# Sliding-window attention with features on the partitions: QK summed by column-tiled selector matmuls, softmax weights spread over the features by DMA

## The chip, the cores and the metric

The kernel runs on one core of one Trainium2 chip. The metric is device time in microseconds (us) of one launch. Every number below comes from the listed runs or from the profile of one execution; "fast" is the state of a run whose time lies within 1.5% of the fastest run of the same kernel.

Engines are named as in the profile: PE (TensorE matmul), PEld (its weight loads), DVE (VectorE), ACT (ScalarE), POOL (GpSimd), SP (SyncE, which issues most DMAs), and the core's 16 DMA engines. A "granted clock" is the TensorE clock that the throttle allowed.

## The reference, cut to what matters

Two layers, each an attention part and a token-mixing MLP, over x of 2048 tokens and 1024 features in bf16. The MLP is not touched by the change.

```python
H = 32; Dh = D // H            # 32 heads of 32 features
W, dil = 8, 2                  # each token sees 8 keys: itself and 7 earlier ones, two apart
qkv = (x @ wqkv) ...           # q, k, v
idx = pos[:, None] - off[None, :]          # off = arange(W) * dil
logits = einsum("bhsd,bhswd->bhsw", q, kg) * scale      # kg = k gathered at idx
logits = where(mask, logits, -1e9)
attn = softmax(logits, axis=-1)
o = einsum("bhsw,bhswd->bhsd", attn, vg)
x = x + o.transpose(...).reshape(B, S, D) @ wo
```

Because the dilation is 2, even and odd tokens never meet in attention. Both kernels treat them as two classes of 1024 tokens each.

## The kernel before

Tokens lie on the partitions (8 per partition and class), and features on the free axis. A chunk is 8 heads of one class; there are 8 chunks a layer. DVE multiplies q with the eight shifted k, then halves the 32 features three times by adds. The rest of that sum, the softmax and the multiplication with v (PV in what follows, as QK is the one with k) follow on DVE too. Because the probability of a token and head lies on the same partition as the features it weights, the multiplication with v reads it through a broadcast along the free axis, without any copy. PE fills DVE's time with projections and MLP matmuls, which an emission loop weaves in between.

```python
def qk(self, ci):                                    # 8 heads (QW = 256 features), 8 tokens a partition
    ...
    for u0 in range(0, W, WB):                       # WB = 2 windows at a time
        nc.vector.tensor_tensor(out=flat, in0=qb, in1=windows(k, u0, WB, [(1, J * QW)]), op=ALU.mult)
        nc.vector.tensor_tensor(out=pr[:, :, 0:16, :], in0=pr[:, :, 0:16, :], in1=pr[:, :, 16:32, :], op=ALU.add)
        nc.vector.tensor_tensor(out=pr[:, :, 0:8, :], in0=pr[:, :, 0:8, :], in1=pr[:, :, 8:16, :], op=ALU.add)
        nc.vector.tensor_tensor(out=St[...], in0=pr[:, :, 0:4, :], in1=pr[:, :, 4:8, :], op=ALU.add)
        yield 0.0, 4.9

def weighted(self, ci, u0, n, dst):                  # PV: the weight is broadcast along the free axis
    v = windows(v_t[ci % 2], u0, n, [(QW, J), (HQ, DH), (1, HQ)])
    pw = Pb[:, u0:u0 + n].unsqueeze(3).to_broadcast([P, n, J, DH, HQ])
    nc.vector.tensor_tensor(out=dst..., in0=v, in1=pw, op=ALU.mult)
```

## Time and profile before

The kernel takes 1396.39 us (median of 4 runs, 1395.99 to 1400.52). The profiled execution spans 1394.9 us.

| Stage | us | PE busy | DVE busy |
|---|---|---|---|
| attention, layer 0 | 0 to 388 | 353 of 388 | 335 of 388 |
| MLP, layer 0 | 388 to 620 | 231 of 232 | 65 |
| attention, layer 1 | 620 to 1066 | 405 of 446 | 364 of 446 |
| MLP, layer 1 | 1066 to 1395 | 325 of 329 | 54 |

The page of the kernel before opens with the busy time of the engines. In the slices, each digit is the busy share of a fortieth of the span, in tenths. The two last lines are the chain of waits that ended last.

```profile
PE 1314.1 (94%) x7840; PEld 749.7 (54%) x7840; DVE 818.0 (59%) x928; ACT 483.4 (35%) x940; POOL 10.5 (1%) x20
...
PE   6999989999899999999899989899949999999998
...
DVE  4869999999820433327999939929976023211111
...
DMA  9423224532342226653365554334206222243531
...
PE 56%; DVE 35%; ACT 6%; issue 2%; DMA 2%; SPq 0%; DVEq 0%; ACTq 0%
```

PE is nearly full everywhere, and in the two attention stages DVE is busy for 86% and 82% as well. A change pays only if it takes work from both there, or moves it to something that has room.

The groups of instructions of the kernel before (busy us, then the mean ns of one) price what the change removes and keeps. L289 and L290 are two of the three QK tree adds, L288 is a QK multiplication (there are two such groups), and L321 a PV multiplication.

```profile
L289 DVE TENSOR_TENSOR T_126<-T_126 128x2048 bf16<-128x2048 bf16 x64 | 78.1, 1221 | 1.2
L288 DVE TENSOR_TENSOR T_126<-q_117,k_119 128x4096 bf16<-128x4096 bf16 x32 | 73.1, 2284 | 4.1 <-PE psg L336 2.2
L321 DVE TENSOR_TENSOR T_126<-v_121,Pb 128x4096 bf16<-128x4096 bf16 (+1 forms) x40 | 73.8, 1864 | 0.9
L290 DVE TENSOR_TENSOR T_126<-T_126 128x1024 bf16<-128x1024 bf16 x64 | 44.0, 688 | 1.4
```

### The profile page before, as it was taken

The numbers are of one execution on the slowest core, as the hardware profiler recorded it, in microseconds if no ns is written. First come the engines' busy times: TensorE is split into PE (matmuls) and PEld (weight loads), VectorE is DVE, ScalarE is ACT, GpSimd is POOL, SyncE is SP. The second block draws the span as 40 slices with busy tenths as digits, with TensorE's granted clock in tenths as the row PEclk, the third lists the DMA queues.
The fourth block names the chain that finished last, engine by engine and source line by source line (L and its number), as shares of the span: only waits on it lengthen the run. The fifth ranks groups of instructions, "written<-read, shape, count | busy, mean of one in ns | idle before, by whom it ended". The sixth has DMA issues, their size and how long they took to land.

```text
span 1394.9 us, 18742 instructions
## 1 busy us (share of the span) xinstructions
PE 1314.1 (94%) x7840; PEld 749.7 (54%) x7840; DVE 818.0 (59%) x928; ACT 483.4 (35%) x940; POOL 10.5 (1%) x20
## 2 busy tenths in 40 slices
PE   6999989999899999999899989899949999999998
PEld 5777656654344444458665458664414444444443
DVE  4869999999820433327999939929976023211111
ACT  7953348633122430013244543475312134100000
POOL 3000000000000000000000000000000000000000
PEclk9999999999999999999999999999969999999999
DMA  9423224532342226653365554334206222243531
GB/s 244 122 72 95 77 66 129 169 94 73 102 136 80 79 72 197 184 156 115 109 172 160 154 162 114 105 102 136 83 16 181 70 81 73 82 137 99 150 99 57
DMA packets 230916, 160.50 MB, mean 115 GB/s; under 512 B 7632, under 2 KB 208336, under 8 KB 230832
## 3 DMA queue, kind: packets, MB, share of 16 engines
q1 hardware_dynamic: 230720, 159.30, 39.3%
q8 instruction: 61, 1.00, 0.3%
q0 software_dynamic: 112, 0.01, 0.1%
q14 instruction: 23, 0.19, 0.0%
HBM read 127.94 MB, written 16.78 MB: 104 GB/s over the span
## 4 chain that ended last, share of the span: by engine, by line
PE 56%; DVE 35%; ACT 6%; issue 2%; DMA 2%; SPq 0%; DVEq 0%; ACTq 0%
PE psg L488 11%; PE pso L488 9%; PE psg L466 9%; DVE T_126 L321 8%; PE ps L273 7%; DVE T_126 L288 7%; PE pso L433 6%; PE pso L466 5%; PE ps L466 4%; DVE T_126 L289 4%; DVE o_q L350 3%; DVE T_126 L349 3%; DVE T_126 L290 2%; DVE St L291 1%; DVE xo L493 1%
## 5 line engine op out<-in xcount | busy, mean ns | idle before, releaser
L433 PE MATMUL pso<-wo,oT 128*128 128x512 bf16 x512 | 121.5, 389 | 0.7 <-DVE xn L439 0.4
L288 DVE TENSOR_TENSOR T_126<-q_116,k_118 128x4096 bf16<-128x4096 bf16 x32 | 73.2, 2289 | 55.5 <-ACT q_116 L275 36.4
L493 DVE SCALAR_TENSOR_TENSOR xo<-psg,b_sb,xs 128x512 bf16<-128x512 f32 x32 | 24.0, 749 | 124.6 <-PE psg L488 124.6
L493 DVE SCALAR_TENSOR_TENSOR xo<-pso,b_sb,xs 128x512 bf16<-128x512 f32 x32 | 24.0, 750 | 103.9 <-PE pso L488 98.6
L433 PEld LDWEIGHTS <-oT 128*128 128x128 bf16 x512 | 50.4, 100 | 62.2 <-issue 7.5
L321 DVE TENSOR_TENSOR T_126<-v_120,Pb 128x4096 bf16<-128x4096 bf16 (+1 forms) x40 | 74.0, 1864 | 11.7 <-PE psg L336 10.8
L289 DVE TENSOR_TENSOR T_126<-T_126 128x2048 bf16<-128x2048 bf16 x64 | 78.1, 1221 | 1.2
L288 DVE TENSOR_TENSOR T_126<-q_117,k_119 128x4096 bf16<-128x4096 bf16 x32 | 73.1, 2284 | 4.1 <-PE psg L336 2.2
L321 DVE TENSOR_TENSOR T_126<-v_121,Pb 128x4096 bf16<-128x4096 bf16 (+1 forms) x40 | 73.8, 1864 | 0.9
L477 DVE TENSOR_TENSOR tmp<-pso,g_132 128x512 f32<-128x512 f32 x4 | 2.8, 692 | 117.0 <-DMA w_10309<-in_B_w_dram 60.7
L273 PE MATMUL ps<-wq,hT_152 128*128 128x256 bf16 x384 | 51.4, 288 | 4.7 <-DMA wq<-in_A_wqkv_dram 2.1
L273 PE MATMUL ps<-wq,hT_6303 128*128 128x256 bf16 x384 | 46.5, 280 | 4.6 <-ACT v_120 L275 4.2
L273 PE MATMUL ps<-wq,hT_4874 128*128 128x256 bf16 x384 | 46.5, 280 | 4.5 <-ACT v_120 L275 4.1
L357 PE MATMUL tpo<-ident,o_q 128*128 128x128 bf16 x256 | 23.9, 235 | 27.9 <-DVE o_q L350 26.2
L358 ACT COPY oT<-tpo 128x1024 bf16<-128x1024 bf16 x32 | 32.3, 1010 | 47.3 <-PE tpo L357 47.3
L273 PE MATMUL ps<-wq,hT_153 128*128 128x256 bf16 x384 | 44.9, 273 | 3.1 <-ACT hT_153 L244 2.5
L273 PEld LDWEIGHTS <-hT_152 128*128 128x128 bf16 x384 | 38.9, 103 | 14.3 <-ACT hT_152 L244 2.9
L273 PE MATMUL ps<-wq,hT_810 128*128 128x256 bf16 x384 | 44.9, 273 | 1.7 <-ACT q_117 L275 1.0
L273 PE MATMUL ps<-wq,hT_811 128*128 128x256 bf16 x384 | 45.5, 273 | 0.4 <-ACT v_120 L275 0.4
L290 DVE TENSOR_TENSOR T_126<-T_126 128x1024 bf16<-128x1024 bf16 x64 | 44.0, 688 | 1.4
L350 DVE TENSOR_TENSOR o_q<-o_q,T_126 128x2048 bf16<-128x2048 bf16 x36 | 44.1, 1225 | 1.2
L349 DVE TENSOR_TENSOR T_126<-T_126 128x2048 bf16<-128x2048 bf16 x36 | 44.1, 1224 | 1.1
(1405 smaller groups left out, 2629.3 us busy)
## 6 DMA issues: line engine op xcount, KB each, us to landing
wq<-in_A_wqkv_dram SPq DMA_DIRECT2D x48, 512.0 KB, 4.2
wo<-in_A_wo_dram SPq DMA_DIRECT2D x64, 128.0 KB, 2.7
xr<-in_A_x_dram SPq DMA_DIRECT2D x16, 256.0 KB, 3.1
out_dram<-xo SPq DMA_DIRECT2D x16, 256.0 KB, 2.2
k_118<-k_118 SPq DMA_DIRECT2D x8, 392.0 KB, 5.0
v_120<-v_120 SPq DMA_DIRECT2D x8, 392.0 KB, 5.0
k_119<-k_119 SPq DMA_DIRECT2D x8, 392.0 KB, 5.0
v_121<-v_121 SPq DMA_DIRECT2D x8, 392.0 KB, 4.9
```

Source lines behind the costliest of these rows:

```text
L273: nc.tensor.matmul(ps[:, jj, :], lhsT=self.hT[c][j // JH][:, kt, j % JH, :], rhs=wts[part][:, kt, :], start=(kt == 0), stop=(kt == KD - 1))
L288: nc.vector.tensor_tensor(out=flat, in0=qb, in1=windows(k, u0, WB, [(1, J * QW)]), op=ALU.mult)
L289: nc.vector.tensor_tensor(out=pr[:, :, 0:16, :], in0=pr[:, :, 0:16, :], in1=pr[:, :, 16:32, :], op=ALU.add)
L290: nc.vector.tensor_tensor(out=pr[:, :, 0:8, :], in0=pr[:, :, 0:8, :], in1=pr[:, :, 8:16, :], op=ALU.add)
L321: nc.vector.tensor_tensor(out=dst.rearrange("p u j (d h) -> p u j d h", h=HQ), in0=v, in1=pw, op=ALU.mult)
L349: nc.vector.tensor_tensor(out=tf[:, 0], in0=tf[:, 0], in1=tf[:, 1], op=ALU.add)
L350: nc.vector.tensor_tensor(out=of, in0=of, in1=tf[:, 0], op=ALU.add)
L358: nc.scalar.copy(out=oT[:, b, :, :], in_=tp[:])
L433: nc.tensor.matmul(ps[:], lhsT=at_.oT[c][kt // 2][:, kt % 2, j, :], rhs=wo_t[n][kt // 4][:, kt % 4, :], start=(kt == 0), stop=(kt == KD - ...
L466: nc.tensor.matmul(ps[:], lhsT=wt[c][:, j, fl * P:(fl + 1) * P], rhs=h2[c][j // JH][:, j % JH, dc * 512:(dc + 1) * 512], start=(k == 0), s ...
L488: nc.tensor.matmul(ps[:], lhsT=w2t[ft // HF][:, ft % HF, c::DIL], rhs=g[ft // GF][:, ft % GF, dc * 512:(dc + 1) * 512], start=(ft == 0), s ...
L493: nc.vector.scalar_tensor_tensor(out=xo[:, dc * 512:(dc + 1) * 512], in0=ps[:], scalar=b2_sb[:, i, c:c + 1], in1=xs[:, dc * 512:(dc + 1) * ...
```

## The change

The intent is to take the QK sum over features away from DVE. Q, K and V are projected transposed: 128 partitions are 4 heads x 32 features, and the tokens lie on the free axis. The product q x k is then summed over features by PE with a 0/1 selector matrix. Four such matmuls of 32 columns each are meant to run side by side in the array. The output comes out transposed as well, so the transposes before the output projection go too.

The price is in the softmax's result. It now lies on one partition per head and token block, but the multiplication with V needs it on each of the head's 32 feature partitions. So the probabilities are written to DRAM (256 KB), and eight DMAs per round ("spreads"), of 1 MB each, read every row back 32 times. A round is 16 heads of one class; there are four rounds a layer. Two buffers hold the spreads.

The diff, cut to its core:

```diff
-        def qk(self, ci):
-            ...
-                nc.vector.tensor_tensor(out=flat, in0=qb, in1=windows(k, u0, WB, [(1, J * QW)]), op=ALU.mult)
-                nc.vector.tensor_tensor(out=pr[:, :, 0:16, :], ..., op=ALU.add)
-                nc.vector.tensor_tensor(out=pr[:, :, 0:8, :], ..., op=ALU.add)
-                nc.vector.tensor_tensor(out=St[...], ..., op=ALU.add)
+        def qk(self, n, dq):                              # dq: one of 4 blocks of 4 heads
+            ...
+            for par in range(2):
+                T = tpl.tile([P, 4, SC], BF16, name="T", tag="T")
+                nc.vector.tensor_tensor(out=T[:], in0=q[:].unsqueeze(1).to_broadcast([P, 4, SC]),
+                                        in1=window(k, par, 2, [(2, 4), (1, SC)]), op=ALU.mult)
+                for sb in range(SB):
+                    for gr in range(4):                   # four column tiles
+                        b = SB * gr + sb
+                        nc.tensor.matmul(self.sc[32 * gr:32 * gr + 32, par], lhsT=sel[:, sb * DQ + dq, :],
+                                         rhs=T[:, :, b * TB:(b + 1) * TB],
+                                         start=(dq == 0 and sb == 0), stop=(dq == DQ - 1 and sb == SB - 1))
+        def softmax_back(self, n):
+            ...
+            nc.sync.dma_start(out=dst, in_=Pb[:].rearrange("p u t -> p (u t)"))      # pd <- Pb, to DRAM
+        def spread(self, n, dq, hf):
+            pb = pbp.tile([P, 4, W, TB], BF16, name="pb", tag="pb")                  # 2 buffers
+            base = self.pd(n)[dq * HD * 4 * SB + 4 * hf, 0]
+            src = bass.AP(base.tensor, base.offset, [(4 * SB * W * TB, HD), (0, DH), (1, 4 * W * TB)])
+            nc.sync.dma_start(out=pb[:].rearrange("p b u t -> p (b u t)"), in_=src)
+        def pv(self, n, dq):
+            for hf in range(2):
+                ...                                       # the spreads of this and the next half are asked for
+                for par in range(2):
+                    half = pb[:, :, 4 * par:4 * par + 4, :]
+                    nc.vector.tensor_tensor(out=half, in0=half, in1=window(v, par, ...), op=ALU.mult)
+                for wd in (4, 2):                         # the sum over windows, in place in pb
+                    nc.vector.tensor_tensor(out=pb[:, :, 0:wd, :], in0=pb[:, :, 0:wd, :], in1=pb[:, :, wd:2 * wd, :], op=ALU.add)
+                nc.vector.tensor_tensor(out=dst, in0=pb[:, :, 0, :], in1=pb[:, :, 1, :], op=ALU.add)
```

The source of a spread has the dimensions 4 heads (`HD`), 32 repeats with stride 0 (`DH`), and 8 KB in a row.

## The prediction

> **What bounds the kernel now.** The page shows PE busy 94% of 1394.9 us, DVE 59%; the chain of waits is PE 56%, DVE 35%. By stage (windows, and the chain in order of time): attention of layer 0 runs to 388 us, of layer 1 from 620 to 1066 us; there both engines are about 95% busy. The MLP stages (388-620, 1066-1391) are PE alone and stay as they are. DMA is 39.7% of 16 engines: 160.5 MB / (0.397 x 16 x 1394.9 us) = 18 GB/s per busy engine.
>
> **What the change does, by the groups' durations.**
> - DVE: the QK tree adds (78.1 + 44.0 + 27.0 us) go; softmax runs twice as wide, half as often (104 to about 51 us); 4 chunks of PV return from PE (+30). The multiplies stay: 64 x 2.29 us for QK, 128 x 1.22 us for PV. Attention DVE: 650 to 505 us, 63 us for each of 8 rounds (a round: 16 heads of one token class).
> - PE: o transposes (24 us) and PV identity sums (128 x 0.216 = 28) go; projections, 3072 x 0.109 us, become 1536 x 0.216: equal. Added: 512 selector matmuls of 32 columns: 110 us one after another; run four together, as the Trainium skill ("TensorEngine Tiling (Array Packing)", Overview) allows, 30 to 75. PE work is about unchanged.
> - ACT: 128 K and V evictions double in length (+55 us); no limit.
> - DMA: 64 spreads of 1 MB come (each probability row to 32 partitions). A round is now softmax, a write to DRAM, then eight spreads in two buffers, each feeding 4.8 us of DVE.
>
> Were the spreads free, PE would bound both attentions at about 360 and 430 us: total about 1365.
>
> **Why I don't expect that.** A spread's DRAM side has the dimensions 4 heads x 32 repeats x 8 KB, 4 outermost. The Trainium skill ("DMA: Bandwidth & Descriptors", on how many engines a DMA uses) says that the engine count is the largest number up to 16 that divides both slowest dimensions: here 4, always the lowest-numbered. No run here shows this yet. Each then moves 256 KB: 14 us at this trace's 18 GB/s, 9 at the page's 27 GiB/s. Estimate: 10 us, 2 to land, plus ordinary traffic on these engines (20 to 30 us a round). A round is also serial between its last PV and the next first spread (PV 4.8, a QK 4.6, softmax 3.6, DRAM write about 3 us). So a round takes 100 to 125 us, against 63 of DVE and 86 (layer 0) or 107 (layer 1) of PE. Layer 0: about 85 us to the first spread, 4 rounds, output projection 28: 500 to 560 us. Layer 1: 510 to 580. Nearly all is critical, as the filler matmuls run out.
>
> **Predicted:** 1620 us, range 1440 to 1760; faster 0.12, same 0.07, slower 0.81.
>
> **What shows each step.** DMA issues: spreads land in over 10 us (under 7 refutes four engines). DVE's PV multiplies, now nearly never waiting, wait for the spread over 150 us in all. PE busy in attention slices falls below 80%. QK adds absent; projection matmuls 0.216 us apart. Eight selector matmuls in under 1.2 us.
>
> **What would make it wrong.** Spreads over 16 engines: then about 1365. A faster engine than 27 GiB/s, or spreads hidden better behind filler: 1440 to 1500. Column tiles that don't overlap: +70 us of PE.

## The result, and the profile after

The changed kernel takes 2032.06 us (median of 4 runs, 2020.79 to 2034.98), against 1396.39 us before in the same rounds. The ratio is 1.452 (95% interval 1.447 to 1.457). Ratios here are the mean time of one kernel's fast runs over that of the other's fast runs of the same rounds, so they are not quite the ratio of the quoted medians. The result is correct. The prediction had the direction right, and its range ended 272 us too low.

The page of the changed kernel, the same lines as before and the granted clock:

```profile
PE 1351.0 (67%) x6305; PEld 588.3 (29%) x6432; DVE 667.2 (33%) x780; ACT 505.4 (25%) x884; POOL 7.3 (0%) x53
...
PE   5943644543741499999654834865639309999999
...
DVE  3522445323322503323341531352133326041111
...
PEclk9986777767875799999877866887869658999999
DMA  6333333334323332464253544233433234223442
...
DMA 44%; PE 37%; DVE 12%; ACT 5%; issue 1%; SPq 1%; DVEq 0%; ACTq 0%
DMA pb<-pd 35%; PE ps L520 16%; PE ps L498 13%; PE ps L287 4%; DVE pb L367 3%; DMA w<-in_B_w_dram 3%; DVE pb L379 3%; DMA xr<-in_A_x_dram 3%; PE ps L465 2%; DMA xr<-xb 2%; DMA pd<-Pb 1%; DVE T L310 1%; PE sc L315 1%; DVE bn L198 1%; DVE oT L381 1%
```

PE does about the same work (1351 us for 1314) and DVE 151 us less, as intended. Yet both are idle through the attention stages, and the chain now runs through DMA for 44% of the span, 35% in the spreads (pb<-pd) alone. The DMA row hovers at 3 in layer 0's attention: this is no shortage of DMA engines in sum.

The busy time by stretch shows where it went. The columns are the stretch, its length, and the busy us of PE, PEld, DVE, ACT and POOL, then the granted clock, the DMA share of 16 engines, and GB/s. The two lines after the header are the four rounds of layer 0 and of layer 1.

```profile
core 0: us, PE busy (x) PEld busy (x) DVE busy (x) ACT busy (x) POOL busy (x), PEclk, DMA share, GB/s
...
90.00:690.00 600.00, 278.90 (x1256) 113.55 (x1280) 220.52 (x223) 129.94 (x216) 0.00 (x0) 0.72 0.35 94
...
992.00:1690.00 698.00, 377.85 (x1736) 159.58 (x1770) 233.37 (x242) 178.21 (x323) 0.00 (x0) 0.77 0.39 107
```

Four rounds take 600 us in layer 0 and 698 us in layer 1: about 150 and 174 us each. PE is busy for 46% and 54% of them. The attention of layer 0 ends at 715 us where it ended at 388, and that of layer 1 takes 770 us (940 to 1710) instead of 446. The MLP stages are a little shorter than before (225 and 320 us for 232 and 329), so the two attentions hold the whole loss, about 325 us each. The low granted clock stands almost only in the slices where PE idles, so I read it as a companion and not as a cause. No run tests that reading alone.

Three groups of the changed kernel price its new operations: the multiplication with V, the selector matmuls, and the QK multiplication. Behind the second bar stands the idle time of the engine just before, and what ended it.

```profile
L367 DVE TENSOR_TENSOR pb<-pb,v 128x2048 bf16<-128x2048 bf16 x96 | 114.8, 1220 | 532.7 <-DMA pb<-pd 532.7
...
L315 PE MATMUL sc<-T,sel 128*32 128x512 bf16 x512 | 44.8, 430 | 227.6 <-DVE T L310 226.4
L310 DVE TENSOR_TENSOR T<-q,k 128x4096 bf16<-128x4096 bf16 x64 | 143.3, 2285 | 83.4 <-ACT q L290 56.5
```

The durations are as costed. The idle time is the news: DVE stood 532.7 us before these 96 multiplications, and a further 198.3 us before the other 32 (731.0 us in all), each time for a spread.

How many engines does a spread use? The DMA view of a window (88 to 150 us, here in 40 slices of 1.55 us) answers. The first line is the share of 16 engines in tenths, and the second is GB/s.

```profile
DMA  3229913222222222226921000027962222222222
GB/s 71 63 72 179 159 39 74 79 63 69 79 85 90 90 95 95 95 102 206 177 51 37 19 1 0 21 63 150 161 102 58 63 74 85 85 95 90 106 100 106
```

While only spreads run, the share is 2 to 3 tenths and the rate 60 to 106 GB/s. Four of sixteen engines are 0.25. The short peaks to 9 are ordinary loads: they are absent in e14 below, where the weight tiles are not loaded. The Trainium skill ("DMA: Bandwidth & Descriptors", section "Why a DMA increments its semaphore by 16 and not by 1") says that the engine count is the largest number up to 16 that divides the slowest dimension of both sides; here these are 4 (the heads, in DRAM) and 128 (the partitions), which gives 4, and this trace agrees.

Next, DVE's own timeline of the changed kernel, in the first round (start us, duration us, and in brackets the idle time before):

```profile
107.94 2.36 DVE L367 TENSOR_TENSOR pb<-pb,v 128x2048 bf16<-128x2048 bf16 x2 [9.62 <-DMA pb<-pd]
120.97 1.22 DVE L367 TENSOR_TENSOR pb<-pb,v 128x2048 bf16<-128x2048 bf16 x1 [10.67 <-DMA pb<-pd]
122.12 1.22 DVE L379 TENSOR_TENSOR pb<-pb 128x2048 bf16<-128x2048 bf16 x1
...
127.18 0.42 DVE L381 TENSOR_TENSOR oT<-pb 128x512 bf16<-128x512 bf16 x1
145.95 2.36 DVE L367 TENSOR_TENSOR pb<-pb,v 128x2048 bf16<-128x2048 bf16 x2 [18.35 <-DMA pb<-pd]
```

The two multiplications of the first spread run at 107.94, but its adds (L379) come only after 122, behind a multiplication that waits 10.67 us for the second spread. In DVE's program the second spread's multiplication stands ahead of the first one's adds, and DVE kept to that order. Since the adds work in place in pb, both buffers come free together, and the next pair of spreads starts only then. The second pair goes the same way. At the third, the adds follow their own multiplications, and SP issues the next spread at 185.66 us, before the pair's other spread has landed at 193.0:

```profile
185.66 12.70 SPq L352 DMA_DIRECT2D pb<-pd  x2
```

By SP's issue times, the next two spreads are asked for within 4 us of each other in 17 of the 24 places where one pair follows another in a round.

That gives the sum of the first round, by the chain of waits in order of time. Its four waits for spreads are these (start us, length us):

```profile
88.58 32.37 DMA pb<-pd
...
127.63 28.61 DMA pb<-pd
...
161.90 31.07 DMA pb<-pd
...
197.83 19.64 DMA pb<-pd
...
243.92 18.50 DMA pb<-pd
```

The waits sum to 111.7 us. Between them lie three stretches of DVE work (6.7, 5.7 and 4.9 us, together 17.2 us). From the end of the fourth wait to the next round's first spread at 243.92 us there are 26.4 us: the last sums, QK, softmax and the write to DRAM. Together that is 155.3 us.

### The profile page after: what moved, and what is told of

Read it like the earlier page. It is cut to its first block, busy times and chain, and to the rows that moved or that the text cites. A ratio compares the mean times of both kernels' runs of the same rounds, so it can differ in the third digit from the quotient of the medians.

```text
span 2030.2 us, 15594 instructions
## 1 busy us (share of the span) xinstructions
PE 1351.0 (67%) x6305; PEld 588.3 (29%) x6432; DVE 667.2 (33%) x780; ACT 505.4 (25%) x884; POOL 7.3 (0%) x53
## 4 chain that ended last, share of the span: by engine, by line
DMA 44%; PE 37%; DVE 12%; ACT 5%; issue 1%; SPq 1%; DVEq 0%; ACTq 0%
DMA pb<-pd 35%; PE ps L520 16%; PE ps L498 13%; PE ps L287 4%; DVE pb L367 3%; DMA w<-in_B_w_dram 3%; DVE pb L379 3%; DMA xr<-in_A_x_dram 3%; PE ps L465 2%; DMA xr<-xb 2%; DMA pd<-Pb 1%; DVE T L310 1%; PE sc L315 1%; DVE bn L198 1%; DVE oT L381 1%
## 5 line engine op out<-in xcount | busy, mean ns | idle before, releaser
L520 PE MATMUL ps<-g,w 128*128 128x512 bf16 x1753 | 401.5, 387 | 85.8 <-DMA w<-in_B_w_dram 83.5
L498 PE MATMUL ps<-h,w 128*128 128x512 bf16 x1755 | 400.2, 386 | 58.5 <-ACT v L293 32.7
L287 PE MATMUL ps<-hT,wq 128*128 128x512 bf16 x1496 | 358.6, 396 | 57.1 <-DMA wq<-in_A_wqkv_dram 49.4
L367 DVE TENSOR_TENSOR pb<-pb,v 128x2048 bf16<-128x2048 bf16 x96 | 114.8, 1220 | 532.7 <-DMA pb<-pd 532.7
L520 PEld LDWEIGHTS <-w 128*128 128x128 bf16 x1792 | 176.5, 99 | 305.0 <-DMA w<-in_B_w_dram 85.5
L498 PEld LDWEIGHTS <-w 128*128 128x128 bf16 x1792 | 176.9, 99 | 280.5 <-issue 54.8
L287 PEld LDWEIGHTS <-wq 128*128 128x128 bf16 x1536 | 152.5, 101 | 257.4 <-DMA wq<-in_A_wqkv_dram 51.2
L465 PE MATMUL ps<-wo,oT 128*128 128x512 bf16 x501 | 131.1, 415 | 143.9 <-DVE oT L381 118.8
L315 PE MATMUL sc<-T,sel 128*32 128x512 bf16 x512 | 44.8, 430 | 227.6 <-DVE T L310 226.4
L310 DVE TENSOR_TENSOR T<-q,k 128x4096 bf16<-128x4096 bf16 x64 | 143.3, 2285 | 83.4 <-ACT q L290 56.5
L379 DVE TENSOR_TENSOR pb<-pb 128x2048 bf16<-128x2048 bf16 (+1 forms) x128 | 121.4, 952 | 1.8
L367 DVE TENSOR_TENSOR pb<-pb,g 128x2048 bf16<-128x2048 bf16 x32 | 38.3, 1221 | 198.3 <-DMA pb<-pd 198.3
L293 ACT CAST k<-ps 128x1024 bf16<-128x1024 f32 x64 | 65.0, 1015 | 49.4 <-PE ps L287 44.1
```

Of the source, the lines that this page charges most:

```text
L287: nc.tensor.matmul(ps[:], lhsT=wt[:, kt, (dt % 2) * P:(dt % 2 + 1) * P], rhs=self.hT[c][hf][:, kt, :], start=(kt == 0), stop=(kt == KD - 1))
L293: nc.scalar.copy(out=window(buf, 0, PADK + hf * HT, [(KW + 1, 2), (1, HT)]), in_=ps[:].unsqueeze(1).to_broadcast([P, 2, HT]))
L310: nc.vector.tensor_tensor(out=T[:], in0=q[:].unsqueeze(1).to_broadcast([P, 4, SC]), in1=window(k, par, 2, [(2, 4), (1, SC)]), op=ALU.mult)
L315: nc.tensor.matmul(self.sc[32 * gr:32 * gr + 32, par], lhsT=sel[:, sb * DQ + dq, :], rhs=T[:, :, b * TB:(b + 1) * TB], start=(dq == 0 and ...
L367: nc.vector.tensor_tensor(out=half, in0=half, in1=window(v, par, 2 + hf * HT, [(TB, 4), (2, 4), (1, TB)]), op=ALU.mult)
L379: nc.vector.tensor_tensor(out=pb[:, :, 0:wd, :], in0=pb[:, :, 0:wd, :], in1=pb[:, :, wd:2 * wd, :], op=ALU.add)
```

## The experiments

Each kernel was timed beside the kernel before on the same chip (1398 to 1400 us there in every set). Unless marked otherwise the result is correct. "Wrong" means that the kernel leaves out data to isolate a cost.

### e1: sixteen engines by cutting the DMA

```diff
-            src = ... [(4 * SB * W * TB, HD), (0, DH), (1, 4 * W * TB)]
-            nc.sync.dma_start(out=pb[:]..., in_=src)
+            for hp in range(HD):                          # one DMA a head: 32 repeats outermost
+                base = self.pd(n)[(dq * HD + hp) * 4 * SB + 4 * hf, 0]
+                src = ... [(0, DH), (1, 4 * W * TB)]
+                nc.sync.dma_start(out=pb[hp * DH:(hp + 1) * DH]..., in_=src)
```

> Each 1 MB spread is cut into four DMAs, one per head (32 repeats of one 8 KB row to 32 partitions): same bytes, same repeated source rows, same queue, four times the issues; only the outermost dimension changes from 4 to 32. Theory A (a spread runs on four of the sixteen engines, and the loads queued behind it on those four suffer too): all sixteen engines share it, a spread lands in 4 to 7 us instead of 14 to 32, DVE's wait for spreads falls from 731 us to under 150, total 1365 to 1450. Rival B (reading one DRAM row 32 times, or 64 MB more through memory, is what is slow): the landing times and the total stay, 1950 to 2050. Rival C (the one issuing queue is the limit, it waits in order for buffers): four times the issues make it slower, over 2050.

Measured: 1502.1 us (1500.16 to 1504.09), ratio 1.072. The same bytes from four DMAs with 32 outermost cost 530 us less. The expected range was missed by 52 us. The DMA view of the same window (88 to 150 us) shows all engines at work:

```profile
DMA  2999999000499899999999990199836999998007
GB/s 77 301 206 217 227 201 196 11 0 0 90 291 211 169 254 222 168 271 244 196 238 183 289 220 0 32 300 260 190 74 192 315 233 201 228 176 179 10 0 222
```

DVE's wait for spreads fell from 731.0 to 88.8 us, as expected (the changed kernel, then e1; us in total, times, longest):

```profile
DVE pb L367 <- DMA pb<-pd: 731.0, 56, 24.6
...
DVE pb L368 <- DMA pb<-pd: 88.8, 27, 14.0
```

The confinement to four engines is the main cause.

### e2: two engines

```diff
+            for g0 in range(0, HD, 2):                    # two DMAs of two heads each
+                src = ... [(4 * SB * W * TB, 2), (0, DH), (1, 4 * W * TB)]
```

> Each spread is cut into two DMAs of two heads each, so the outermost dimension is 2: same bytes, twice the issues. Theory A: two engines per DMA, the same two for all, so a spread takes twice as long (about 28 us per 1 MB against 14): 64 x 14 = 900 us more, total 2700 to 3000. B and C: within 100 us of 2032, because bytes and rows are the same and the issues only double.

Measured: 2434.96 us (one run, state unknown), in the expected direction and some 270 us short of the expected range; why it is short was not looked into. In the window the share falls to a tenth, at about half the changed kernel's rate:

```profile
DMA  3011111111111111169111111111113931000011
GB/s 82 16 32 32 32 32 32 37 42 32 37 37 42 53 53 53 53 206 162 50 53 53 53 53 53 53 53 53 53 48 107 232 76 38 19 10 0 0 11 42
```

Two of sixteen engines are 0.125; from 92 to 112 us, where no peak falls, the share is 0.13. With 16, 4 and 2 engines the time is 1502, 2032 and 2435 us.

### e3: no spread at all (wrong)

```diff
-            nc.sync.dma_start(out=pb[:]..., in_=src)
+            # nothing is read; PV multiplies V with a constant tile of 1/8
```

> Wrong on purpose: no spread at all, PV reads a constant tile of 1/8 and writes to a buffer of its own; every matmul, every DVE and ACT operation and the DRAM write of the softmax stay. It measures the rest of the change by itself. My prediction said 1365 for free spreads (layer 0 attention 360 us, layer 1 430). If the total is 1340 to 1400, the whole loss of 636 us comes from the spreads; if it is above 1450, the transposed layout itself (selector matmuls, weave, five PSUM buffers) costs too.

Measured: 1356.72 us (1356.05 to 1357.32), ratio 0.969. This is the floor of the new layout in this order of work: QK by selectors is worth 3% if the spread is free. The prediction had put it at about 1365 us.

### e4: another queue, same shape

```diff
-            nc.sync.dma_start(out=pb[:]..., in_=src)
+            nc.gpsimd.dma_start(out=pb[:]..., in_=src)
```

> The spreads are issued from the POOL queue, shapes unchanged, so SP's loads no longer wait in order behind a spread that waits for its buffer. Theory A, if the engines were the same four: the spread still needs 13 us or more, total 1800 to 2000; if the POOL queue deals out its four engines in turn (the Trainium skill says that of software-generated DMAs), two spreads in flight run side by side: 1450 to 1650. Rival C (order on the SP queue): under 1450 with spreads that land in under 10 us.

Measured: 2011.95 us (one run, state unknown). Taking the spreads out of SP's queue changes next to nothing, and the time lies just above the range for four engines (1800 to 2000). In the window from 88 to 150 us this queue's packets took 35.3% of 16 engines, which is 5.6 engines on average, so more than four took part. That fits what the expectation draws from the Trainium skill ("DMA: Bandwidth & Descriptors", section "Why a DMA increments its semaphore by 16 and not by 1"), engines dealt out in turn, though no view shows which engines they were. But the packets were slow: 4.20 MB / (0.353 x 16 x 62 us) = 12 GB/s per busy engine. The spreads issued there landed after a median of 25.7 us. So the order in SP's queue is not the main cause, and whether spreads that use other engines at the full rate would help can't be read from this run.

### e5 and e6: e1 from another queue

```diff
-                nc.sync.dma_start(out=pb[hp * DH:(hp + 1) * DH]..., in_=src)
+                nc.gpsimd.dma_start(...)      # e5;   e6: nc.scalar.dma_start(...)
```

> Cut per head as in e1_heads1 (sixteen engines), and issued from the POOL queue instead of SP's. In e1 the weight loads stood behind up to sixteen spread issues in SP's queue (88 to 110 us) and PE waited 78 us for weights. Theory D (what e1 still loses, 145 us against no spread, is order on one queue): most of it comes back, 1370 to 1430, PE's wait for wq and w loads under 30 us. Rival E (bandwidth: 64 MB more through engines that are already 76% busy in attention): little changes, 1480 to 1520. In e4 the POOL queue moved its bytes in smaller packets, so E may even be 1520 to 1600.

> The same with ACT's hardware queue. ACT waits in order for a free buffer before each issue, so its evictions stand behind that wait, but the packets stay as large as SP's. D: 1390 to 1470 (the gain of a queue of its own, less what ACT's evictions lose). E: 1480 to 1550. If it is slower than e1 while e5 is faster, ACT's own order is the reason.

Measured: 1458.29 us (1452.46 to 1459.27) for POOL and 1484.96 us (1478.46 to 1487.19) for ACT, against 1502.1 for SP. With 16 engines the shared queue does cost: 44 us in POOL's favour, 17 in ACT's. POOL's time lies between the ranges of D and E, so order holds a part and not most of it; ACT's lies just above D's range, in E's. With POOL, DVE then waits 134.3 us for Q and 79.2 for spreads.

### e7: e1 with half the bytes (wrong)

```diff
-                src = ... [(0, DH), (1, 4 * W * TB)]
+                src = ... [(0, DH), (1, 2 * W * TB)]      # the other half of pb keeps a constant
```

> Wrong on purpose: e1 with every spread moving only the first half of its bytes (4 KB instead of 8 KB per partition, the other half holds a constant), all issues, waits and order unchanged, on SP. E (bandwidth): half of the 145 us comes back or more, 1400 to 1440. D (order, and the latency of each issue): 1470 to 1500, since nothing in the order changes. In between: both.

Measured: 1382.8 us (1379.24 to 1383.82), ratio 0.988, 119 us under e1, more than the expectation had for bandwidth (1400 to 1440). The bytes themselves cost time even with 16 engines: of the 145 us between e1 and the floor of e3, half the bytes hold 119.

### e8 and e9: is it the repeated row, or the partitions?

Their outputs are wrong, which doesn't matter for the times.

```diff
-                base = self.pd(n)[(dq * HD + hp) * 4 * SB + 4 * hf, 0]; src = ... [(0, DH), (1, 4 * W * TB)]
+                base = self.pd(n)[0, 0];  src = ... [(4 * W * TB, DH), (1, 4 * W * TB)]    # e8: 32 different rows
+            src = ... [(992, P), (1, 4 * W * TB)]         # e9: one DMA, 128 overlapping rows, 128 outermost
```

> Wrong on purpose: e1 (four DMAs per spread, one per head, to 32 partitions each, on SP), but the 32 partitions read 32 different rows of 8 KB of the round's softmax tensor instead of one row 32 times. Bytes, issues, destinations and order as in e1. In e1 the busy engines moved only about 14 GB/s each. Rival G (reading one row over and over is slow): 1400 to 1450. Theory F (32 destination partitions reach only 8 of the 16 memory ports, as the Trainium skill says of SBUF, so the DMA tops out near 200 GB/s): unchanged, 1490 to 1515.

> Wrong on purpose: the spread is one DMA again, on SP, its outermost dimension is 128 partitions on both sides (overlapping rows of the softmax tensor, 1 MB in all). F: all sixteen engines and all sixteen ports, a spread lands in about 4.5 us or less, DMA moves over 300 GB/s while spreads run, total 1390 to 1440. If bytes are bytes (neither G nor F): near e1, 1480 to 1510. It differs from e1 in two ways, ports and a quarter of the issues; e10 and e8 bracket it.

Measured: e8 takes 1501.7 us (1498.27 to 1506.14), equal to e1, so reading one row 32 times is no problem in e1's form. e9 takes 1403.38 us (1397.69 to 1405.21), 99 us less than e1, and its spreads of 1 MB land in 6.0 us (median; about 4.5 was expected):

```profile
DMA  5999930000059999940049999988628982900000
GB/s 130 375 381 428 332 101 0 11 0 0 0 126 281 386 386 423 290 138 0 0 95 412 323 385 418 309 177 328 275 63 338 354 252 55 280 10 0 0 0 0
```

In the slices with a share of 9, e1 moved 234 GB/s on average (168 to 315, 25 slices) and e9 360 (280 to 428, 16 slices). The Trainium skill ("SBUF — State Buffer", section "Door 1: The DMA port swizzle") says that partitions 0 to 31 reach only 8 of the 16 SBUF ports, and gives 189 GB/s for them and 328 GB/s for 128 partitions, both at 1 MiB. The pair e1 and e9 agrees with that in direction: DMAs onto 32 partitions are slower than one onto 128, at the same share of engines. Both rates lie above the page's figures; these slices hold ordinary loads too. The pair also differs in one DMA for four, so the ports were not isolated.

### e10 and e11: more rows in DRAM, fewer repeats

```diff
+            for r in range(8): nc.sync.dma_start(...)      # each softmax row is written 8 times
-            src = ... [(4 * SB * W * TB, HD), (0, DH), (1, 4 * W * TB)]
+            src = ... [(4 * SB * W * TB, HD * 8), (0, DH // 8), (1, 4 * W * TB)]    # 32 rows x 4 repeats
```

> A correct kernel that should get what e9 gets: each softmax row is written to memory eight times (eight writes of 256 KB a round instead of one), so that a spread's memory side is 32 rows x 4 repeats and one DMA reaches all engines and ports. F: like e9 plus the extra writes (16 MB in all, 5 to 8 us more in the chain of each round): 1410 to 1470. If over 1500, replication costs more than the ports give.

> e10 with the spreads issued from the POOL queue, so that SP's weight loads are not behind them (that gave 44 us between e1 and e5). F and D together: 1375 to 1430. Below 1385 it would beat the kernel before; no spread at all measured 1357.

Measured: 1446.05 us (1442.65 to 1450.16) from SP and 1465.61 us (1463.06 to 1473.85) from POOL. One DMA of 32 rows onto all 128 partitions, and correct: 56 us better than e1. The POOL version was a miss. What helped e1 by 44 us harmed here by 20; its trace shows DVE waiting 187.2 us for spreads instead of 144.3. Why the queue that was better for small DMAs is worse for large ones stays open.

### e12: half the spreads

```diff
-  lhsT=wt[:, kt, (dt % 2) * P:(dt % 2 + 1) * P]
+  lhsT=wt[:, kt, dt % 2::2]          # 8 heads x 16 features in a block: one spread serves two blocks
+  src = ... [(4 * SB * W * TB, 2 * HD * RP), (0, GR // RP), (1, 4 * W * TB)]    # 16 rows (2 copies) x 8 repeats
+  pw = tpl.tile([P, 4, W, TB], BF16, name="pw", tag="T")     # the product has its own tile
```

> A correct kernel meant to beat both: each projection matmul takes every second column of its weight tile, so that a block of 128 features holds 8 heads x 16 features instead of 4 x 32. One spread then serves two blocks: 32 spreads of 1 MB instead of 64, and the products go to a buffer of their own. Each softmax row is written twice, so a spread's memory side is 16 rows x 8 repeats: sixteen engines. Half the bytes as in e7_half_bytes (1383), but with a quarter of e7's issues and wider reach over the memory ports: 1360 to 1385, that is 1 to 3% under the kernel before. No spread at all was 1357. If the strided weight columns slow the weight loads (98 ns each so far, hidden under matmuls of 216 ns), or the second spread of a round comes late: 1390 to 1430.

Measured: 1414.55 us (1410.57 to 1417.5), ratio 1.010. The bytes are halved with a correct result, yet the time missed the expectation of 1360 to 1385 us. DVE waits only 66.9 us for spreads, but 175.0 us for Q: in one place, 98 to 138 us, PE ran 184 projection matmuls in a row while DVE had no QK to do.

### e13: the changed kernel with half the bytes, still four engines (wrong)

```diff
-            src = ... [(4 * SB * W * TB, HD), (0, DH), (1, 4 * W * TB)]
+            src = ... [(4 * SB * W * TB, HD), (0, DH), (1, 2 * W * TB)]
```

> The changed kernel with half the bytes in each spread (512 KB, still one DMA over 4 heads x 32 repeats, so still 4 engines); wrong result on purpose. Theory A (the mis-sized term is the transfer time of a spread on 4 engines, 14 to 16 us per MB instead of the 10 predicted): 64 spreads lose 7 to 8 us each and nearly all of it is on the chain: 1520 to 1600 us. Theory B (most of a round's excess is ordinary loads and waits in the queue, which don't shrink with the bytes): above 1750 us.

Measured: 1685.68 us (1682.02 to 1692.65). The result lies between the two theories and decides for the bytes. With none, half and all of them, the time is 1356.72, 1685.68 and 2032.06 us: steps of 329 and 346 us, nearly a straight line. The expectation of more, 7 to 8 us for each of the 64 spreads, took all of a transfer to be on the chain; it saved 346 / 64 = 5.4 us each.

### e14: the changed kernel without the repeated weight loads (wrong)

```diff
-                t = wqp.tile(...); nc.sync.dma_start(out=t[:], in_=wq_v[...])
+                t = wq_c[part]                      # three tiles, loaded once, used throughout
```

> The changed kernel with the QKV weight tiles loaded three times in all and then used again (24 MB of ordinary loads less; wrong result on purpose). If the ordinary loads that share the 4 engines and the queue carry part of the excess (estimate: 3 MB a round over 16 engines at about 18 GB/s is 10 us a round, 80 us in all, plus PE's 49 us of waits for these tiles): 1900 to 1960 us. If they carry nothing that the chain shows: above 2010 us.

Measured: 2013.48 us (2003.44 to 2016.03), 19 us less, the second of the two cases expected: 24 MB of QKV weight loads on the same engines and in the same queue carry almost nothing. Other ordinary loads were left in (see the account below). The trace is worth more than the time, because here the spreads run nearly alone in the first round. Its DMA view from 88 to 248 us, in slices of 4 us:

```profile
DMA  2222220002222220022222100222221000002122
GB/s 59 66 84 94 100 96 29 2 16 72 66 74 90 104 92 14 20 70 80 88 96 102 59 8 25 68 68 78 88 96 74 29 0 0 4 0 66 39 63 78
```

Four engines work for some 26 us, then stand idle for about 8, pair by pair. The chain gives 27.70, 28.14, 25.90 and 19.41 us of waits for the four pairs. A pair is 2 MB, so its first wait is 14 us per MB, or 2.10 MB / 27.7 us / 4 = 19 GB/s per engine. The idle stretches are the buffers that come free together.

### e15 and e16: putting e12's order right

```diff
+                    nxt = qk_proj(n, 1) if half == 0 else qk_proj(n + 1, 0) if n < last else iter(())
...
-                        yield from self.pv(n - 1, 2 * half)
-                        yield from self.pv(n - 1, 2 * half + 1)
+                        for unit in chain(self.pv(n - 1, 2 * half), self.pv(n - 1, 2 * half + 1)):
+                            yield unit
+                            yield from islice(nxt, 2)          # e15: the next projections, two after each sum
```

In e16 `softmax_back(n)` (and so the write to DRAM) moves between the two sums of the second half, and the first spreads go before the next round's first QK.

> The correct variant of e12 (1414.6 us) with the next half's K and Q projections woven into the weighted sums, two after each unit, instead of following them. If the order of the projections, for which DVE waited 175 us in e12, holds the rest: DVE's wait for Q falls below 80 us and the time is 1375 to 1400 us. If PE's sum of work and the spreads hold it: 1405 to 1420 us.

> e15 and also the second half of the softmax, its write to DRAM and the first spreads issued one step earlier (before the next round's first QK). If the serial path softmax, write, spread, sum still shows in e15: 15 to 30 us under e15, 1350 to 1385 us, which would beat the kernel before by up to 3%. If DVE never waits there: equal to e15 within 0.5%.

Measured: e15 1397.59 us (1395.39 to 1402.26), ratio 0.999; e16 1380.82 us (1377.97 to 1384.72), ratio 0.987 with an interval of 0.984 to 0.990. In e15 the wait for Q fell from 175.0 only to 113.1 us (under 80 was expected), but the time is in the range. In e16 the wait for spreads fell from 51.7 to 23.0 us, and this is the first correct version that beats both kernels: by 1.3% over the kernel before. The waits of e16 (us in total, times, longest):

```profile
DVE T L314 <- ACT q L294: 118.7, 14, 22.2
...
DVE pw L366 <- DMA pb<-pd: 23.0, 9, 7.3
```

What is left to the floor of 1357 us is 24 us; whether the wait for Q holds it was not tested.

### e17 and e18: freeing the buffer before the adds

```diff
+                pw = tpl.tile([P, 4, W, TB], BF16, name="pw", tag="T")
-                    nc.vector.tensor_tensor(out=half, in0=half, in1=window(v, ...), op=ALU.mult)
+                    nc.vector.tensor_tensor(out=pw[:, :, 4 * par:4 * par + 4, :], in0=half, in1=window(v, ...), op=ALU.mult)
...                                                   # the adds work in pw
```

e17 makes this edit in the changed kernel, e18 in e1.

> The changed kernel with the PV product in a tile of its own, so that a spread's buffer comes free after its two multiplies; spreads and their 4 engines unchanged, correct result. The trace of e14 shows why: DVE's program puts the adds of spread A behind the multiply that waits for spread B, so both buffers come free together and the four engines stand idle 8 to 10 us after each pair. If that is the rest of the mis-sized term: three such gaps of about 7 us a round go, 8 rounds: 1840 to 1900 us, and a round of about 130 us. If only the transfer itself counts: above 1990 us.

> The same edit on e1 (four DMAs of one head each, 16 engines, 1502 us). There DVE's trace shows the adds directly behind their own multiplies in nearly every sum, so the early release should buy at most the adds' 2.4 us where DVE waited for a spread (27 waits): 1450 to 1500 us. Equal to e1 within 0.5% if ordinary loads and partitions hold it.

Measured: e17 1906.86 us (1891.86 to 1913.57), 125 us under the changed kernel and 7 us above the expected range; e18 1488.11 us (1486.31 to 1489.68), 14 us under e1 and inside its range. One tile, with bytes, engines and queue unchanged, gives 125 us back. DVE's whole wait for spreads in e17:

```profile
  DMA pb<-pd: 492.0, 51
```

It was 731.0 us. DVE's wait for Q rose from 56.5 to 178.9 us at the same time, so of 239 us less waiting for spreads 125 reached the time. The shape of the DMA is still the larger loss: e1 gained 530 us.

## Why the prediction was right or wrong

- "Were the spreads free, PE would bound both attentions ... total about 1365." Right: e3 measured 1356.72 us.
- "QK tree adds go", multiplies stay at 2.29 and 1.22 us, "eight selector matmuls in under 1.2 us". Right: the adds are gone, the multiplications take 2.285 and 1.220 us, and the 512 selector matmuls are busy for 44.8 us, 0.70 us for eight. The Trainium skill ("TensorEngine Tiling (Array Packing)", Overview) says that the array can work as independent tiles; one after another, the prediction's estimate for the 512 was 110 us, so they overlap.
- "the engine count is ... here 4". Right, by the share of about 0.25 in the changed kernel, and by e1 and e2, which moved the count up and down and the time with it.
- DVE waits for spreads "over 150 us in all", PE "below 80%" in attention. Right in direction: 731 us, nearly five times as much, and 46% and 54%.
- "about 85 us to the first spread ... output projection 28". Right: 88.58 us, and about 25 us in layer 0 (690 to 715).
- "So a round takes 100 to 125 us". Wrong, and this is the step that failed. A round took 150 us in layer 0 and 174 in layer 1. The middle of the predicted range is 112 us; (150 - 112 + 174 - 112) x 4 = 400 us. By stage, the attentions took 715 and 770 us, 185 and 225 us over the middles of "500 to 560" and "510 to 580": about the whole of the 412 us between 1620 and 2032. The four engines and the wait for spreads were right. What failed is the overlap in this term: it set the path of the spreads beside the work of DVE and PE ("against 63 of DVE and 86 ... or 107 ... of PE"). The spreads cost 2032 - 1357 = 675 us, and the prediction gave them 1620 - 1365 = 255, which is 32 a round.

The writes of the softmax to DRAM (`pd<-Pb` in SP's timeline), one a round, show what the spreads cost in each round. The time from one write to the next, in us:

| | layer 0 | layer 1 |
|---|---|---|
| changed kernel | 156.9, 145.8, 152.9 | 159.1, 216.6, 175.0 |
| e13, half the bytes | 112.4, 109.4, 113.6 | 127.8, 170.7, 136.2 |
| e3, no spread | 73.7, 66.3, 75.0 | 75.7, 135.0, 94.2 |
| changed kernel less e3 | 83, 80, 78 | 83, 82, 81 |

The spreads cost 78 to 83 us in every round, whether the round without them takes 66 us or 135, and half the bytes cost about half of that (42 on average). So most of their time (8 spreads of 14 us are 112) was added to the other work of a round, and no more of it was hidden in a long round than in a short one. Layer 1's rounds are longer than layer 0's with or without spreads.

The term had four parts, and the runs show what became of each:

- The transfer. "Estimate: 10 us" for a spread leaned on the skill's figure of 27 GiB/s, though the same sentence worked out 14 us from the trace of the kernel before. In e14, where the spreads run nearly alone, it is 14 us. That is 8 x 4 = 32 us a round if none of it is hidden. The waits of e14's first round sum to 101.2 us, where the prediction had 8 x 10 + 2 = 82.
- The ordinary traffic, "20 to 30 us a round". Oversized for the QKV weights: taking away these 24 MB saved 19 us in all (e14). In the first round it shortened the four waits from 111.7 to 101.2 us. Together with the transfer the prediction had 102 to 112 us here, so in the first round these two errors cancelled, which is luck.
- The double buffer. Not in the prediction: it took the two buffers for an overlap of transfer and sums. The trace has 17.2 us of sums between the waits of the first round. In the first two of the three stretches (12.4 us) the DMA engines are idle (share 0.05 and 0.06), because the adds stand behind the wait for the pair's other spread; in the third the next spread is already under way (0.26). e17 gave 125 us back, on average 16 us for each of the 8 rounds.
- The serial end of a round: about 16 us by the prediction's own four numbers, 26.4 us in the first round's chain. In layer 1 the chain there also passes through MLP matmuls and normalisations woven into this stretch: 36 us from the end of the last spread wait at 1118.0 to the next spread's issue at 1153.9 us. No experiment shortened this stretch in the changed kernel, so its share of the loss is read from the trace and not shown.

One effect is not in the prediction at all: other ordinary loads wait behind the spreads. The line of the chain above gives some 7% of the span (3.1, 2.8 and 1.5% before rounding), 150 us, to waits for MLP weights (`w`) and residual tiles (`xr`). Two of its pieces (start us, length us), and PE's waits for such tiles in the changed kernel (us in total, times, longest):

```profile
1214.88 27.96 DMA w<-in_B_w_dram
...
1368.49 30.74 DMA xr<-xb
...
PE ps L520 <- DMA w<-in_B_w_dram: 83.5, 4, 33.4
...
PE ps L468 <- DMA xr<-in_A_x_dram: 46.9, 4, 20.5
```

PE's waits for all ordinary loads sum to 250 us here and to about 4 us in e3, where there are no spreads. The second interval of layer 1 holds 63 us of such waits on the chain and lost no more than the others (82 us), so they seem to stand in place of waits for spreads; no run tests that alone.

The prediction's own parts also sum to more than the middle of its range: 8 x 10 + 2 + 20 to 30 + 16 is 118 to 128 us, and 85 + 4 x (100 to 125) + 28 is 513 to 613 us for layer 0, where it wrote 500 to 560. Both sums were rounded down.

## What to carry to other kernels

Look at the outermost dimension of every large DMA before costing its bytes, and cost them at the rate that your own trace shows: a broadcast written as 4 rows x 32 repeats ran on 4 engines, and the same bytes with 32 outermost took 530 us off this kernel. A second buffer overlaps transfer and work only if the consumer lets go of the first one early: keep in-place work off a buffer that a DMA is to refill, and read in the timeline which instruction really frees it. Do not take a transfer for hidden because other engines have work meanwhile: here most of it was added to every round, 81 us on average. When a layout gains on one engine but needs a costly broadcast, measure the floor without it first (3% here), then look for a layout in which one broadcast serves twice and starts early, as e12 and e16 did.

## What the Trainium skill lacked or had wrong

- "DMA: Bandwidth & Descriptors", Specifications, gives about 27 GiB/s per engine. Four engines reading 8 KB rows from DRAM gave 19 GB/s each over the whole wait for a pair of spreads (e14), and 26 in the best slices (104 GB/s over four). The measurement decides. In each pair the rate climbs from about 60 to 100 GB/s; why stays open.
- The same page says how the engine count is chosen for a DMA, and the shares of e14 (0.25 from 90 to 112 us) and of e2 (0.13 from 92 to 112 us) agree. It has no figure for what POOL's queue moves per engine with such a shape: 12 GB/s in e4.
- "SBUF — State Buffer", section "Door 1: The DMA port swizzle": e1's 234 GB/s at full share onto 32 partitions a DMA, and e9's 360 GB/s onto 128, agree with it in direction only. The page has no figure for four DMAs onto the four groups of 32 partitions, queued one after another: e1's 234 GB/s, ordinary loads included, is such a case.
- No page has the trap of e17: an engine whose program interleaves in-place work on two buffers frees both at about the same time, and the DMAs that refill them wait. Undoing it gave 125 us of 2032 back.
